# VectorE's stream transpose in place of TensorE's transposes of K and P in a decode block with an 8192-key cache

## The chip, the cores and the metric

One core of one Trainium2 chip runs the whole kernel. The metric is device time in microseconds (us) of one execution. The five engines named below are TensorE (PE in the profile, with PEld for its weight loads), VectorE (DVE), ScalarE (ACT), GpSimd (POOL) and SyncE (SP). Each has its own in-order instruction stream, and they meet through semaphores.

## What is computed

One decode step of a transformer block, for 4 sequences with one new token each. The part that matters here is attention over a cache of 8192 keys for 32 heads of 128 channels:

```python
x: (4, 1, 512); k_cache, v_cache: (4, 32, 8192, 128), all bf16
q = layernorm(x) @ wq                         # per sequence and head: 128 numbers
scores = einsum("bhqd,bhkd->bhqk", q, k_cache) * 128 ** -0.5
p = softmax(scores)
o = einsum("bhqk,bhkd->bhqd", p, v_cache)
h = x + o.reshape(4, 1, 4096) @ wo
out = h + (sigmoid(layernorm(h) @ w_gate) * (layernorm(h) @ w_up)) @ w_down
```

The caches are 128 (sequence, head) pairs of K and V, 2 MB each, 512 MB of K and V in all. Each byte is used once, for one query. "Head" stands for such a pair below, n = 0 to 127.

## The kernel before, in words

**Loads.** SP issues every load (L276 to L304). K or V of one head is one DMA of 2 MB into one of eight slots of the tile `KV` (`NSL`): partition p holds keys 64p to 64p+63, 16 KB in a row. The list `order` (L307 to L314) fixes the sequence: K of head n beside V of head n-9 (`LAGH`), the query weights `wq` behind K 0, four pieces of `wo` behind K 2 to K 5, and the feed-forward weights near and behind the last V. A load into a slot waits until the slot's former holder is used up: a K after its last transpose (`t_tr`), a V after its last product (`t_pv`). `pump` puts loads on SP's queue as soon as that event exists in program order.

**Order of the work.** A loop over u counts quarters of heads (u = 4n + s). In each step it emits the transposes of quarter s of head n, what is due of the softmax chain, the scores of an earlier step, and `pv` of the quarter 36 steps back. Each `emit` appends to one engine's stream with its waits.

**Scores.** The product q.K needs the channels on the partitions, and K arrives with keys there. So `transposes` (L359 to L375) reads K as 32-bit words (two bf16 channels in one word), and TensorE transposes 128x128 words at a time, 32 per head (L364), through four PSUM banks. ScalarE (L373) and VectorE (L375) take turns to copy 128x512 words to the tile `kTc`. `scores` (L377 to L396) then runs, for the even and the odd channel of each word, four products with 32 weight columns each, side by side on the four column strips of the array (L389): 16 for a head. The weights are windows of `Lq`, zero but for q in one column, so that 8 heads (a group, `GH`) collect their scores in different rows of one PSUM bank.

**Softmax.** For each of 16 groups: a copy of the bank to `S_sb` (L403), a maximum over keys (L405, L410 to L425, which go through TensorE for the steps across partitions), the exponential on ScalarE (L427), the sum and the scaling (L433 to L436). Then four TensorE products with the identity transpose P (L443) and VectorE scatters it to `PT` (L451). The chain's steps are emitted 4, 6, 9 and 13 quarter steps behind the group's last scores.

**Output.** `pv` (L458 to L492) multiplies P into V, again on four column strips (L473), for the last group in another form (L485); `finish` and `project` sum the strips (L512, L520) and multiply by `wo` (L502). Behind the loop stand a layer norm and the feed-forward part (L610 to L626) and one small store of the output (L636).

Of the kernel before, what the change touches and what calls it, by code (L numbers as in the profile page):

```python
# [5 lines left out]
BF16 = mybir.dt.bfloat16  # L6
FP32 = mybir.dt.float32
# [5 lines left out]
NTB = 4  # L13
NKT = 8
# [63 lines left out]
def bass_sequential_preLN__mha_block_cached__glu_gated_glu__decode_kernel(  # L78
# [20 lines left out]
    NT = R // 8  # L99
# [4 lines left out]
    W = 64  # L104
# [4 lines left out]
    with ExitStack() as es:  # L109
# [18 lines left out]
        q2 = SB("q2", [128, 2, NH], BF16)  # L128
        Lq = SB("Lq", [128, 2, 2, GH, W], BF16)
        KV = SB("KV", [128, NSL, R * 128], BF16)  # L130
        kTc = SB("kTc", [128, NKT, 512], FP32)
        S_sb = SB("S_sb", [128, 512], FP32)
# [31 lines left out]
        bankT = bank[0:4]  # L164
        SBK, OBK, XS, XO = 4, 5, 6, 7
# [52 lines left out]
        def f_xT(e):  # L218
# [15 lines left out]
            bass.AP(raw(M8), 0, [[GH, 128], [0, 16], [1, GH]])), [t_m8])  # L234

# [110 lines left out]
        t_sev = {}  # L346
# [6 lines left out]
        KVW = KV[:, :, :].bitcast(FP32)  # L353
        kTb = kTc[:, :, :].bitcast(BF16)

        def transposes(n, t):
            g = n * NT + t
            slot = slot_of["k", n]

            def f(e):  # L360
                ins = None
                for i in range(4):
                    c = 128 * (4 * t + i)
                    ins = e.transpose(bankT[g % NTB][:, 128 * i:128 * (i + 1)], KVW[:, slot, c:c + 128], identf[:, :])  # L364
                return ins
            tok = emit("pe", f, [t_k[n][t // 2], t_identf, t_copy.get(g - NTB)])
            if t == NT - 1:
                t_tr[n] = tok

            ks = g % NKT  # L370
            w = [tok, t_score.get(n * 2 + t // 4 - 2)]
            if g % 2 == 0:
                t_copy[g] = emit("act", lambda e: e.copy(kTc[:, ks, :], bankT[g % NTB][:, :]), w)  # L373
            else:
                t_copy[g] = emit("dve", lambda e: e.tensor_copy(kTc[:, ks, :], bankT[g % NTB][:, :]), w)  # L375

        def scores(u):  # L377
            n, m = u // 2, u % 2
            g, i = n // GH, n % GH
            first = i == 0 and m == 0  # L380
            last = i == GH - 1 and m == 1
            off = 31 - (16 * m + i)

            def f(e):
                mms = []
                for par in range(2):
                    for j in range(4):
                        ks = (n * NT + 4 * m + j) % NKT
                        mms.append(e.matmul(PS[32 * j:32 * (j + 1), 512 * SBK:512 * (SBK + 1)],  # L389
                                            Lq[:, g % 2, par, i, off:off + 32], kTb[:, ks, par:par + 1023:2],  # L390
                                            start=first and par == 0, stop=last and par == 1,
                                            tile_position=(0, 32 * j)))
                return mms[4:] if last else mms[-1]
            w = [t_copy[n * NT + 4 * m + j] for j in range(4)] + [t_lq[g]]
            if first and g:
                w.append(t_sev[g - 1])  # L396
            t_score[u] = emit("pe", f, w, incs=4 if last else 1)
# [3 lines left out]
        def softmax(g):  # L401

            t_sev[g] = emit("act", lambda e: e.activation(S_sb[:, :], bank[SBK], ACT.Copy),  # L403
                            [t_score[16 * g + 15], st_.get("exp")])
            t_mx = emit("dve", lambda e: e.tensor_reduce(mpart[:, :], S_sb[:, :], AX.X, ALU.max),  # L405
                        [t_sev[g], st_.get("p1")])
# [14 lines left out]
            def p2():  # L421
                t = emit("pe", lambda e: e.matmul(  # L422
                    bank[XS][:, 128:129], rowpad[:, :], identf[:, 0:1], start=True, stop=True),
                    [box["d2"], t_rp0])
                a1 = emit("dve", lambda e: e.tensor_scalar(  # L425
                    negmb[:, :], bank[XS][:, 128:129], -SCALE, None, op0=ALU.mult), [t, st_.get("exp")])
                box["a2"] = emit("act", lambda e: e.activation(  # L427
                    E_sb[:, :], S_sb[:, :], ACT.Exp, bias=negmb[:, 0:1], scale=SCALE, accum_out=sig[:, 0:1]),
                    [a1, st_.get("ptr")])
                st_["exp"] = box["a2"]  # L430

            def p3():
                t = emit("pe", lambda e: e.matmul(  # L433
                    bank[XS][:, 130:131], Gmat[:, :], sig[:, 0:1], start=True, stop=True), [box["a2"], t_gm])
                d3 = emit("dve", lambda e: e.reciprocal(rsum[:, :], bank[XS][:, 130:131]), [t])
                box["d4"] = emit("dve", lambda e: e.tensor_scalar(  # L436
                    E_sb[:, :], E_sb[:, :], rsum[:, 0:1], None, op0=ALU.mult), [d3, box["a2"]])

            def p4():
                def f(e):  # L440
                    ins = None
                    for q in range(4):
                        ins = e.matmul(bank[XS][:, 128 * q:128 * (q + 1)], E_sb[:, 128 * q:128 * (q + 1)],  # L443
                                       ident[:, :], start=True, stop=True)
                    return ins
                t = emit("pe", f, [box["d4"]])
                st_["ptr"] = t
                pb = g % 2
                dst = bass.AP(raw(PT), pb * NK * GH * 32, [[2 * NK * GH * 32, 128], [GH * 32, NK], [36, GH], [1, 4]])
                src = bass.AP(raw(PS), XS * 512, [[4096, 128], [GH, NK], [1, GH], [128, 4]])  # L450
                st_["xs"] = t_ptc[g] = emit("dve", lambda e: e.tensor_copy(dst, src),  # L451
                                            [t, t_pt0, t_pvg.get(g - 2)])
            return [(4, p1), (6, p2), (9, p3), (13, p4)]

        def pcol(g, i, t, r2):
            kk = 4 * (t % 4) + 2 * (t // 4) + r2
            return g % 2, (kk * GH + i) * 32

        def pv(n, m):
# [5 lines left out]
            if first and g:  # L465
                w.append(t_oev[g - 1])
            if g < NG - 1:
                def f(e):
                    mms = []
                    for j in range(4):  # L470
                        t, r2 = 2 * m + j // 2, j % 2
                        pb, o = pcol(g, i, t, r2)
                        mms.append(e.matmul(PS[32 * j:32 * (j + 1), 512 * OBK:512 * (OBK + 1)], PT[:, pb, o:o + 32],  # L473
                                            in_slot(slot, [[256, 4], [1, 128]], (8 * t + r2) * 128),
# [3 lines left out]
            else:  # L478
                def f(e):
                    ins = None  # L480
                    for r in range(16 * m, 16 * (m + 1)):
                        q = r % 8 // 2
                        pb, o = pcol(g, i, r // 8, r % 2)
                        o += 4 * i + q
                        ins = e.matmul(bank[OBK][:, i:i + 1], KV[:, slot, 128 * r:128 * (r + 1)],  # L485
# [24 lines left out]
        def finish(g):  # L510
            ob = g % 2
            t_oev[g] = emit("act", lambda e: e.activation(O_sb[:, :], bank[OBK], ACT.Copy),  # L512
# [19 lines left out]
        def q_projection():  # L532
# [12 lines left out]
            def f2(e):  # L545
                ins = None
                for par in range(2):
                    for lo in (0, 64):
                        ins = e.matmul(bank[XO][lo:lo + 64, NH * par:NH * (par + 1)], ident[:, par:par + 127:2],
                                       q_all[:, :], start=True, stop=True, tile_position=(0, lo))  # L550
                return ins
            t2 = emit("pe", f2, [tq, t_ident])
            st_["q"] = st_["xo"] = emit("dve", lambda e: e.tensor_copy(
                q2[:, :, :].rearrange("p e n -> p (e n)"), bank[XO][:, 0:2 * NH]), [t2])
# [3 lines left out]
        def q_windows(g):  # L558
            w = [st_["q"], t_lq0, t_score.get(16 * (g - 1) - 1)]
            for r2 in range(2):  # L560
                lo = 64 * r2
                t_lq[g] = emit("dve", lambda e, lo=lo, r2=r2: e.tensor_copy(  # L562
                    Lq[lo:lo + 64, g % 2, :, :, 31 + 8 * r2], q2[lo:lo + 64, :, GH * g:GH * (g + 1)]), w)


        for u in range(4 * (NH + LAGH)):
            n, s = u // 4, u % 4
            for q in range(4):
                if n < NH and q % 2 == 0:
                    transposes(n, 2 * s + q // 2)  # L570
# [6 lines left out]
            if u > 3 and u % 2 == 0 or u == 3:  # L577
                su = u // 2 - 1
                if su < 2 * NH:
                    scores(su)  # L580
                    if su % 16 == 15:
                        if su // 16 + 2 < NG:
                            q_windows(su // 16 + 2)
                        for d, fn in softmax(su // 16):
# [13 lines left out]
        t_ot = emit("dve", lambda e: e.tensor_copy(OT[:, gl % 2, :], bank[OBK][:, 0:GH]),  # L598
# [17 lines left out]
        t_u = emit("pe", glu_mm(t_w["wu"][0], bank[SBK]), [t_hn, t_w["wu"][1], t_sev[gl]])  # L616
        t_hh = emit("dve", lambda e: e.tensor_tensor(hhT[:, :], sg_sb[:, :], bank[SBK][:, 0:NF], ALU.mult), [t_sg, t_u])
# [3 lines left out]
        for i in range(2):  # L621
            def f_down(e, i=i):
                ins = None
                for t in range(half * i, half * (i + 1)):
                    for c in range(NDC):
                        ins = e.matmul(cols(bank[OBK], c), wd_v[:, t, 128 * c:128 * (c + 1)],  # L626
# [5 lines left out]
            h2T[:, :], sth[:, 0:NDC * B], bank[OBK][:, 0:NDC * B], ALU.add), [t_d, st_["h"]])  # L632
# [61 lines left out]
```

## Time and profile before

| | us |
|---|---|
| median of three runs (lowest, highest) | 1312.22 (1311.79, 1312.52) |
| the profiled execution's own time | 1311.99 |
| its span, first to last instruction | 1310.2 |
| TensorE busy | 1029.1, 9293 products and as many weight loads |
| of it, transposes of K (L364) | 664.6, 4096 products |
| VectorE busy | 410.8, 715 instructions |
| ScalarE busy | 335.6, 583 instructions |

Loads move 550.8 MB. The page's rows of engines give the share of the span in which an engine was at work; the row of DMA gives in tenths how busy the 16 DMA engines were in each of 40 slices. "Idle before, releaser" of a group of instructions says how long its engine stood idle ahead of it and what ended that. A granted clock (PEclk) of 1.00 is TensorE's full speed.

### The profile page before, as it was taken

The page shows a single profiled execution, that of the slowest core. Times are in us where ns is not written, and L with a number is a line of the kernel's source. Part 1 is how long each engine was busy: PE and PEld are TensorE (multiplying, and loading weights), DVE is VectorE, ACT ScalarE, POOL GpSimd, SP SyncE. Part 2 cuts the span into 40 slices and gives each one's busy share as a digit, 9 for nine tenths or more (in the row PEclk, how much of TensorE's full clock was granted, in tenths as well). Part 3 has the DMA queues.
Part 4 walks back from the last instruction along what each step waited for, and adds up shares of the span by engine and source line. Part 5 has one row for each costly group of instructions (what it writes and reads, how often), then busy time and mean ns, then how long its engine had stood idle before and what let it go on. Part 6 is the DMA issues. An engine that isn't in the chain of part 4 may idle for free.

```text
span 1310.2 us, 20596 instructions
## 1 busy us (share of the span) xinstructions
PE 1029.1 (79%) x9293; PEld 661.5 (50%) x9293; DVE 410.8 (31%) x715; ACT 335.6 (26%) x583; POOL 9.9 (1%) x11
## 2 busy tenths in 40 slices
PE   5887877887878788878788788787787878878864
PEld 4554544555545455555555455454454555445543
DVE  4442323323233232322323233232232323323310
ACT  1332322222222222222223223222222322222210
POOL 3000000000000000000000000000000000000000
PEclk7998888888888888888888889799798988888865
DMA  9999999999999999999999999999999999999996
GB/s 378 420 426 429 427 428 427 427 428 425 428 427 427 428 427 426 427 429 425 428 427 427 427 427 427 427 429 426 428 426 428 428 427 427 427 428 425 429 421 260
DMA packets 45471, 552.11 MB, mean 421 GB/s; under 512 B 4420, under 2 KB 10312, under 8 KB 12360
## 3 DMA queue, kind: packets, MB, share of 16 engines
q1 hardware_dynamic: 45384, 550.79, 99.3%
q8 instruction: 74, 1.21, 0.4%
q14 instruction: 13, 0.11, 0.0%
HBM read 550.77 MB, written 0.00 MB: 420 GB/s over the span
## 4 chain that ended last, share of the span: by engine, by line
DMA 80%; PE 17%; SPq 2%; ACT 1%; DVE 0%; issue 0%
DMA KV<-in_A_v_cache_dram 75%; PE PS L364 10%; PE PS L473 3%; DMA KV<-in_B_w_down_dram 2%; PE PS L389 2%; DMA KV<-in_A_k_cache_dram 1%; DMA Wreg<-in_A_wq_dram 1%; SPq L279 1%; ACT E_sb L427 0%; DVE kTc L375 0%; SPq L304 0%; PE PS L410 0%; PE PS L433 0%; PE PS L443 0%; PE PS L422 0%
## 5 line engine op out<-in xcount | busy, mean ns | idle before, releaser
L364 PE MATMUL PS<-identf,KV 128*128 128x128 f32 x4096 | 664.6, 311 | 12.8 <-DMA KV<-in_A_k_cache_dram 11.2
L364 PEld LDWEIGHTS PS<-identf,KV 128*128 128x128 f32 x4096 | 518.1, 159 | 192.7 <-issue 152.5
L375 DVE COPY kTc<-PS 128x512 f32<-128x512 f32 x512 | 356.1, 699 | 737.1 <-PE PS L364 736.6
L373 ACT COPY kTc<-PS 128x512 f32<-128x512 f32 x512 | 300.3, 586 | 883.2 <-PE PS L364 883.2
L473 PE MATMUL PS<-KV,PT 128*32 128x512 bf16 x1920 | 215.6, 439 | 223.8 <-DMA KV<-in_A_v_cache_dram 223.8
L473 PEld LDWEIGHTS PS<-KV,PT 128*32 128x32 bf16 x1920 | 51.8, 98 | 346.1 <-DMA KV<-in_A_v_cache_dram 278.8
L389 PE MATMUL PS<-kTc,Lq 128*32 128x512 bf16 x2048 | 177.7, 426 | 1.7 <-DVE Lq L562 1.0
L389 PEld LDWEIGHTS PS<-kTc,Lq 128*32 128x32 bf16 x2048 | 32.2, 97 | 50.4 <-issue 32.0
L485 PE MATMUL PS<-PT,KV 128*128 128x1 bf16 x512 | 15.1, 165 | 17.3 <-DMA KV<-in_A_v_cache_dram 15.1
L485 PEld LDWEIGHTS PS<-PT,KV 128*128 128x128 bf16 x512 | 14.4, 104 | 17.9 <-DMA KV<-in_A_v_cache_dram 15.6
L520 PE MATMUL PS<-selq,O_sb 128*128 128x8 f32 x120 | 16.7, 266 | 3.5 <-ACT O_sb L512 3.5
L520 PEld LDWEIGHTS PS<-selq,O_sb 128*128 128x128 f32 x120 | 15.3, 200 | 7.3 <-ACT O_sb L512 7.3
L451 DVE CAST PT<-PS 128x512 bf16<-128x512 f32 x16 | 11.1, 692 | 23.9 <-PE PS L443 23.9
L427 ACT ACTIVATE E_sb<-S_sb,negmb 128x512 bf16<-128x512 f32 x16 | 11.6, 724 | 22.4 <-DVE negmb L425 22.4
L414 DVE TENSOR_REDUCE mrow<-PS 1x8 f32<-1x128 f32 x16 | 4.5, 278 | 30.9 <-PE PS L410 30.9
L405 DVE TENSOR_REDUCE mpart<-S_sb 128x1 f32<-128x512 f32 x16 | 11.0, 686 | 4.9 <-ACT S_sb L403 4.9
L512 ACT ACTIVATE O_sb<-PS 128x512 f32<-128x512 f32 x15 | 9.0, 598 | 12.0 <-PE PS L473 12.0
L403 ACT ACTIVATE S_sb<-PS 128x512 f32<-128x512 f32 x16 | 9.6, 597 | 9.1 <-PE PS L389 9.1
L598 DVE CAST OT<-PS 128x8 bf16<-128x8 f32 x1 | 0.2, 167 | 32.0 <-PE PS L485 32.0
L207 ACT ACTIVATE lnw<-lnw 128x4 f32<-128x4 f32 x2 | 0.4, 206 | 38.1 <-DVE lnw L204 38.1
L433 PE MATMUL PS<-sig,Gmat 128*128 128x1 f32 x32 | 7.3, 297 | 3.7 <-ACT E_sb L427 3.5
L433 PEld LDWEIGHTS PS<-sig,Gmat 128*128 128x128 f32 x32 | 6.6, 258 | 6.8 <-ACT E_sb L427 6.6
(70 smaller groups left out, 124.8 us busy)
## 6 DMA issues: line engine op xcount, KB each, us to landing
KV<-in_A_k_cache_dram SPq DMA_DIRECT2D x127, 2048.0 KB, 28.3
KV<-in_A_v_cache_dram SPq DMA_DIRECT2D x127, 2048.0 KB, 32.9
Wreg<-in_A_wq_dram SPq DMA_DIRECT2D x4, 1024.0 KB, 11.7
Wreg<-in_A_wo_dram SPq DMA_DIRECT2D x4, 1024.0 KB, 14.6
KV<-in_A_k_cache_dram SPq DMA_DIRECT2D x4, 512.0 KB, 5.7
KV<-in_A_v_cache_dram SPq DMA_DIRECT2D x4, 512.0 KB, 26.1
KV<-in_B_w_gate_dram SPq DMA_DIRECT2D x1, 1792.0 KB, 28.0
KV<-in_B_w_up_dram SPq DMA_DIRECT2D x1, 1792.0 KB, 25.9
```

What stands on the lines that cost most here:

```text
L279: done[n] = [prog.dma("sp", f"sl{slot}", lambda e: e.dma_start(KV[:, slot, :], src), w)] * 4
L364: ins = e.transpose(bankT[g % NTB][:, 128 * i:128 * (i + 1)], KVW[:, slot, c:c + 128], identf[:, :])
L373: t_copy[g] = emit("act", lambda e: e.copy(kTc[:, ks, :], bankT[g % NTB][:, :]), w)
L375: t_copy[g] = emit("dve", lambda e: e.tensor_copy(kTc[:, ks, :], bankT[g % NTB][:, :]), w)
L389: mms.append(e.matmul(PS[32 * j:32 * (j + 1), 512 * SBK:512 * (SBK + 1)], Lq[:, g % 2, par, i, off:off + 32], kTb[:, ks, par:par + 1023:2] ...
L405: t_mx = emit("dve", lambda e: e.tensor_reduce(mpart[:, :], S_sb[:, :], AX.X, ALU.max), [t_sev[g], st_.get("p1")])
L427: box["a2"] = emit("act", lambda e: e.activation(E_sb[:, :], S_sb[:, :], ACT.Exp, bias=negmb[:, 0:1], scale=SCALE, accum_out=sig[:, 0:1]), ...
L433: t = emit("pe", lambda e: e.matmul(bank[XS][:, 130:131], Gmat[:, :], sig[:, 0:1], start=True, stop=True), [box["a2"], t_gm])
L451: st_["xs"] = t_ptc[g] = emit("dve", lambda e: e.tensor_copy(dst, src), [t, t_pt0, t_pvg.get(g - 2)])
L473: mms.append(e.matmul(PS[32 * j:32 * (j + 1), 512 * OBK:512 * (OBK + 1)], PT[:, pb, o:o + 32], in_slot(slot, [[256, 4], [1, 128]], (8 * t ...
L485: ins = e.matmul(bank[OBK][:, i:i + 1], KV[:, slot, 128 * r:128 * (r + 1)], PT[:, pb, o:o + 1], start=(r == 0), stop=(r == R - 1))
L520: ins = e.matmul(bank[XO][:, 0:GH], O_sb[:, 128 * q:128 * (q + 1)], selq[:, q:q + 29:4], start=(q == 0), stop=(q == 3))
```

## The change

K's transposes go to VectorE. Its stream transpose turns blocks of 32x32 words within groups of 32 partitions, from SBUF to SBUF: one instruction takes a quarter of a head, 128x1024 words, straight from the slot to `kTc`, which now has four buffers. PSUM and the two copying engines are no longer on that way. Since the blocks stay in their group of 32 partitions, each group a holds the channels of its own keys: a product needs q repeated in the four groups, each with its own output column. So `Lq` gets windows of 128 columns with four live ones, at 32a + 8s + i for quarter s and head i of the group, and a quarter's scores are four products over the whole array (word half c, channel parity e), 16 for a head as before. `q_windows` now fills two heads at a time with one product by a mask (`amask`); the repeated q comes from a selection matrix (`selrep`). Scores of two groups alternate between two PSUM banks, `S_sb` and its copy go, and the maximum and the exponential read the bank. P's transpose is a stream transpose on VectorE as well, from `E_sb` straight into `PT`. `pv`'s products keep their number and shape; they alternate between two banks and take other rows of V, in the order of the new P. Loads, slots and `order` stay as they are.

```diff
-NTB = 4
-NKT = 8
+NKT = 4
...
+        def transposes(n, s):
+            u = 4 * n + s
+            slot = slot_of["k", n]
+            t_copy[u] = emit("dve", lambda e: e.transpose(
+                kTc[:, u % NKT, :], KVW[:, slot, 64 * RC * s:64 * RC * (s + 1)]), [t_k[n][s], t_score.get(u - NKT)])
+            if s == 3:
+                t_tr[n] = t_copy[u]
...
-                for i in range(4):
-                    c = 128 * (4 * t + i)
-                    ins = e.transpose(bankT[g % NTB][:, 128 * i:128 * (i + 1)], KVW[:, slot, c:c + 128], identf[:, :])
-                return ins
-            tok = emit("pe", f, [t_k[n][t // 2], t_identf, t_copy.get(g - NTB)])
...
-                t_copy[g] = emit("act", lambda e: e.copy(kTc[:, ks, :], bankT[g % NTB][:, :]), w)
-            else:
-                t_copy[g] = emit("dve", lambda e: e.tensor_copy(kTc[:, ks, :], bankT[g % NTB][:, :]), w)
...
+                for ce in range(4):
+                    ins = e.matmul(sbank(g), Lq[:, n // QH % 2, n % QH, ce, off:off + 128],
+                                   k3[:, :, ce // 2, :, ce % 2], start=first and ce == 0, stop=last and ce == 3)
...
-                for par in range(2):
-                    for j in range(4):
-                        ks = (n * NT + 4 * m + j) % NKT
-                        mms.append(e.matmul(PS[32 * j:32 * (j + 1), 512 * SBK:512 * (SBK + 1)],
-                                            Lq[:, g % 2, par, i, off:off + 32], kTb[:, ks, par:par + 1023:2],
...
-            t_sev[g] = emit("act", lambda e: e.activation(S_sb[:, :], bank[SBK], ACT.Copy),
-                            [t_score[16 * g + 15], st_.get("exp")])
-            t_mx = emit("dve", lambda e: e.tensor_reduce(mpart[:, :], S_sb[:, :], AX.X, ALU.max),
-                        [t_sev[g], st_.get("p1")])
+            t_mx = emit("dve", lambda e: e.tensor_reduce(mpart[:, :], sbank(g), AX.X, ALU.max),
+                        [t_score[32 * g + 31], st_.get("p1")])
...
-                    for q in range(4):
-                        ins = e.matmul(bank[XS][:, 128 * q:128 * (q + 1)], E_sb[:, 128 * q:128 * (q + 1)],
-                                       ident[:, :], start=True, stop=True)
...
-                st_["xs"] = t_ptc[g] = emit("dve", lambda e: e.tensor_copy(dst, src),
-                                            [t, t_pt0, t_pvg.get(g - 2)])
+                dst = bass.AP(raw(PT), pb * NK * GH * 32, [[2 * NK * GH * 32, 128], [GH * 32, NK], [1, 4], [36, GH]])
+                t_ptc[g] = emit("dve", lambda e: e.transpose(dst, E_sb[:, :]),
+                                [box["d4"], t_pt0, t_pvg.get(g - 2)])
...
+            t_lq[k] = emit("dve", lambda e: e.tensor_tensor(dst, src, keep, ALU.mult),
+                           [st_["q"], t_lq0, t_am, t_score.get(4 * QH * (k - 1) - 1)])
```

## The prediction, on record before the result was seen

> **What bounds the kernel now.** I read the page's rows of engines and DMA first, since they say whether any engine is full.
>
> ```profile
> PE 1029.1 (79%) x9293; PEld 661.5 (50%) x9293; DVE 410.8 (31%) x715; ACT 335.6 (26%) x583; POOL 9.9 (1%) x11
> ...
> DMA  9999999999999999999999999999999999999996
> ...
> DMA packets 45471, 552.11 MB, mean 421 GB/s; under 512 B 4420, under 2 KB 10312, under 8 KB 12360
> q1 hardware_dynamic: 45384, 550.79, 99.3%
> q8 instruction: 74, 1.21, 0.4%
> ...
> DMA KV<-in_A_v_cache_dram 75%; PE PS L364 10%; PE PS L473 3%; DMA KV<-in_B_w_down_dram 2%; PE PS L389 2%; DMA KV<-in_A_k_cache_dram 1%; DMA Wreg<-in_A_wq_dram 1%; SPq L279 1%; ACT E_sb L427 0%; DVE kTc L375 0%; SPq L304 0%; PE PS L410 0%; PE PS L433 0%; PE PS L443 0%; PE PS L422 0%
> ```
>
> No engine is full; the DMA engines are. The 10% of L364 in the chain is only the way by which a landed slot is handed back to SP. Next, whether a faster hand-back would help: the waits of SP, and the median time from issue to landing.
>
> ```profile
> SPq L279 <- PE PS L473: 1108.4, 120, 14.9
> ...
> SPq L279 <- PE PS L364: 32.8, 12, 9.6
> ...
> KV<-in_A_v_cache_dram SPq DMA_DIRECT2D x127, 2048.0 KB, 32.9
> ```
>
> SP does wait for slots, but what it issues lands 32.9 us later, while the landings of single 2 MB loads follow each other by 4.89 us: some six loads are always queued, so an earlier hand-back only lengthens the queue, and a later one costs nothing until it is some 15 us late (the queue less the lag of the slowest DMA engine, below). One head is a K and a V, so **the period is 9.78 us**.
>
> The same two rows hide what can still move. The table of stages at the end of the span shows a queue that does not drain evenly:
>
> ```profile
> 1280.00:1285.00 5.00, 0.00 (x0) 0.00 (x0) 0.00 (x0) 0.00 (x0) 0.00 (x0) 0.50 1.04 423
> 1285.00:1290.00 5.00, 1.87 (x64) 1.78 (x64) 0.00 (x0) 0.00 (x0) 0.00 (x0) 0.50 0.92 365
> 1290.00:1295.00 5.00, 2.88 (x96) 2.72 (x96) 0.00 (x0) 0.00 (x0) 0.00 (x0) 0.50 0.57 229
> 1295.00:1300.00 5.00, 2.14 (x42) 1.80 (x42) 1.45 (x9) 0.43 (x2) 0.00 (x0) 0.50 0.74 271
> ```
>
> The last two columns are the busy share of the 16 DMA engines and GB/s: in the last 20 us only about half of them work. The trace has 16 landings for each load, one for each DMA engine. Around 20 us they lie within 1.2 us of each other; at 64 us within 2.3 us, at the end within 15 us. By then eight engines lie 12.8 to 15.0 us behind the first, the other eight at most 6.7 us. The packet records say why: queue 8 ("instruction") brings one 16 KB packet about every 18 us, 1.06 us each, where a 16 KB packet of K or V takes 0.613 us. TensorE's stream is 2 x 9293 = 18586 instructions; 1.21 MB is 65 bytes for each, so this is **TensorE's program being fetched**. A single engine's lag jumps by about 1.35 us at such a packet, in turn on eight engines, and never shrinks: the K/V packets take 0.613 us on every engine, and still do when half of the engines have run dry. A load counts as landed with its sixteenth part, so these eight engines set the end: w_down lands at 1306.6 us, and 0.9 us of products, the sum, a small product, a copy and the store follow.
>
> **The change part by part.** TensorE loses 4096 transposes and 64 products for P, each with a weight load: 2 x 4160 = 8320 of 18586 instructions (45%). Scores stay at 2048 and pv at its number. Its program shrinks by 0.542 MB, 33 packets. Price of one: between span times 64 and 1116 us the mean lag of the eight late engines grew from 1.43 to 12.42 us over 57 packets, 0.193 us each, or 6.4 us for 33. By the single jump it is 1.35/8 = 0.169, 5.6 us; by the packet's own 1.06 us alone 0.133, 4.4 us. I take **5.8 us**, near the middle of the upper two, since the jump holds more than the packet. The other engines' lag of 6.7 us caps the gain at 15.0 - 6.7 = 8.3 us. ScalarE's 528 fewer instructions are fetched in 8 KB packets on queue 14, ten in the whole steady part: nothing that ends last.
>
> VectorE drops 512 copies (356.1 us) and gets 512 transposes of 128x1024 words. The trace shows none. The nearest rows:
>
> ```profile
> L375 DVE COPY kTc<-PS 128x512 f32<-128x512 f32 x512 | 356.1, 699 | 737.1 <-PE PS L364 736.6
> L436 DVE TENSOR_SCALAR E_sb<-E_sb,rsum 128x512 bf16<-128x512 bf16 x16 | 5.7, 354 | 0.6
> L228 DVE TENSOR_REDUCE M<-identf 128x8 f32<-128x128 f32 x1 | 0.4, 377 | 0.0
> L543 DVE CAST q_all<-PS 128x128 bf16<-128x128 f32 x1 | 0.3, 291 | 8.2 <-PE PS L537 8.2
> ```
>
> From 128 to 512 words a copy grows by 699 - 291 = 408 ns, 1.06 ns a word, with about 0.155 us fixed: 1.24 us for 1024 words. The quickest row (bf16 from SBUF, 354 ns) gives 0.39 ns an element, so 0.55 us; the slowest per element, the strided reduction, (377 - 155)/128 = 1.73 ns, so 1.93 us. I take 1.24 us, the row of the same words into the same tile, so 5.0 us a head. The rest of VectorE's work: the softmax of a group (0.69 + 0.28 + 0.21 + 0.15 + 0.17 + 0.35 us, some 0.7 for P's scatter, which stays one instruction), 0.33 for the outputs, and four window products of about 0.2 us: 3.7 us for 8 heads. In-order waits within that chain were 1.9 (L414), 1.4 (L435) and 1.5 us (L525) a group. That is 8.5/8 = 1.1 us a head, so VectorE needs 6.1 us of the 9.78 (3.3 to 8.8 by the bounds): hidden by the DMA queue. Its cover is gone where 4T + 1.1 = 9.78, at T = 2.2 us.
>
> The Trainium skill ("VectorE: DVE Perf Modes", The three transpose paths) speaks against the change: it gives 311 ns for a VectorE transpose of 128x128 bf16. Taken eight times for 1024 columns that is an estimate of 2.5 us, 11.1 us a head, and VectorE would bound the kernel. But a 128-column copy already takes 291 ns in this trace, mostly fixed; with 20 ns more for 128 columns the estimate becomes 1.4 us, 6.7 us a head.
>
> TensorE's new scores are 16 whole-array passes of 512 columns a head. A pass over four strips now takes 0.32 us at full clock (eight L389 in 0.64 us) and 0.52 us at half (1.04 us). A whole-array product reads the same columns at the same stride, so I take the same: 5.1 to 8.3 us, with 1.6 to 2.5 us of pv (0.40 or 0.62 us for four L473). Before it was 32 transposes (1.09 or 1.97 us for eight), 4.4 to 7.9 us, with 1.3 to 2.1 of scores and the same pv: 7.3 to 12.5 before, 6.7 to 10.8 after. TensorE gets a little lighter at either clock, and the granted mean is 0.852 now. No gain or loss at the end.
>
> Moved waits: K's slot is now freed by VectorE's fourth transpose. Ahead of it on VectorE stand the maximum (waiting for the group's last scores) and the chain's steps, some 8 us once in eight heads, inside the 15 us that the queue forgives. Behind a transpose that waits for K stand the next softmax steps; all wait for loads in the order of `order`, so none waits for a later one. ScalarE's copy of the scores (0.6 us) leaves the chain, off the path. At the start K 0's transposes end before the last of wq lands (20.3 us), even behind the 5.4 us copy at L232 and the new constants; `wo` waits for the q products as before, with 4 MB of K queued. Sum: 0 at the start, 0 a head, 0 behind the last landing, -5.8 in the lag.
>
> **Rivals.** *The fetch does not decide* (14%): the lag has another source, or the freed time on the eight engines is lost again, since w_down's second half is issued for 16.3 us against a full queue. Then 1311 to 1313 us, that is, unchanged. Against it stands that jumps and packets come one by one. *VectorE becomes the bound* (11%), the other side: a transpose of 32-bit words that needs two passes, 2 x 1.06 x 1024 ns + 0.155 = 2.33 us. Then 10.4 us a head, 0.64 over the period, times some 120 heads behind the first slots: +77 less the 5.8, about 1383 us. It decides from T = 2.2 us on; just above that (2.25 us, 10.1 us a head) it costs 120 x 0.32 = 38 us. For it: no row shows the instruction. Against it: every row of plain 32-bit moves is one pass. A half clock that keeps TensorE at 10.8 us a head is no separate case: before, 12.5 us at half clock did not bind.
>
> **How the numbers follow.** The forecast (75%) is the profiled 1311.99 - 5.8 = 1306.2 us; that execution lies 0.2 us below the median of 1312.22. Its own range is 1303.7 (the cap) to 1308.5 (4.4 us, less a packet's step of about 1 us on the last engine). The range of 8 in 10 adds the no-change case: 1303.5 to 1313. About 0.2%, 2.6 us, is what a measurement of this kernel can tell from no change: faster 0.75, within 0.14, slower 0.11.
>
> **What would show it.** Right: about 41 packets on the instruction queue, the last landings some 8 us apart instead of 15, a DMA share near 1 for longer at the end, VectorE near 680 us (410.8 - 356.1 + 512 x 1.24) and transposes near 1.24 us. Wrong: transposes over 2.2 us, SP waiting for VectorE with a DMA row that shows gaps, or the spread at the end unchanged with fewer packets.

## The result, and the profile after

The changed kernel takes 1307.20 us (median of six, 1306.93 to 1307.51) where the kernel before, on the same chip, takes 1311.82 (1311.58 to 1312.52): a ratio of 0.9964, 95% interval 0.9951 to 0.9977. The profiled execution went from 1311.99 to 1307.25 us, its span from 1310.2 to 1305.1.

The page after: busy time of each engine, DMA packets by queue, and the two new groups of VectorE with the scores of TensorE.

```profile
PE 883.7 (68%) x5133; PEld 283.5 (22%) x5133; DVE 682.3 (52%) x750; ACT 27.4 (2%) x55; POOL 10.3 (1%) x11
...
DMA  9999999999999999999999999999999999999997
...
q1 hardware_dynamic: 45384, 550.79, 99.8%
q8 instruction: 40, 0.66, 0.2%
q14 instruction: 9, 0.07, 0.0%
...
L372 DVE STREAM_TRANSPOSE kTc<-KV 128x1024 f32<-128x1024 f32 x512 | 606.1, 1225 | 446.0 <-DMA KV<-in_A_k_cache_dram 445.1
L391 PE MATMUL PS<-kTc,Lq 128*128 128x512 bf16 x2048 | 650.8, 448 | 14.5 <-DVE kTc L372 12.6
...
L440 DVE STREAM_TRANSPOSE PT<-E_sb 128x512 bf16<-128x512 bf16 x16 | 37.3, 2333 | 0.0
```

The DMA row is as full as before, and SP still waits for slots long before its loads could be late; only the engine that frees a K slot has changed (first lines of SP's waits):

```profile
SPq L293 <- DVE kTc L372: 611.2, 122, 11.9
SPq L293 <- PE PS L461: 494.5, 119, 7.1
```

What has changed is the end. In the table of stages (the last two columns are the busy share of the DMA engines and GB/s) they stay full 5 us longer than before and the uneven rest is short:

```profile
1280.00:1285.00 5.00, 1.87 (x64) 1.78 (x64) 0.00 (x0) 0.00 (x0) 0.00 (x0) 0.50 1.01 416
1285.00:1290.00 5.00, 2.80 (x96) 2.71 (x96) 0.00 (x0) 0.00 (x0) 0.00 (x0) 0.50 1.01 389
1290.00:1295.00 5.00, 2.22 (x45) 1.80 (x42) 1.08 (x7) 0.00 (x0) 0.00 (x0) 0.50 0.83 299
1295.00:1300.00 5.00, 3.79 (x136) 3.71 (x137) 0.77 (x5) 1.71 (x3) 0.00 (x0) 0.50 0.70 235
```

The instruction queue brings 40 packets in place of 74. The sixteen landings of the last quarter of V 127, the last load of the cache, lie 8.6 us apart instead of 14.9. But the first of them comes at 1283.4 us instead of 1281.5: the early engines have become 1.9 us later, and 1.5 us of this is there by 94 us. So w_down lands at 1301.46 instead of 1306.60 us, 5.1 us earlier: 6.3 us won from the lag, 1.9 lost ahead of it, and 0.7 won between this load and w_down. The loss was not in the prediction, so the runs below ask two things: whether the length of TensorE's program is the cause of the gain, and where the loss sits.

### The profile page after: what moved, and what is told of

Read it like the earlier page. It is cut to its first block, busy times and chain, and to the rows that moved or that the text cites. A ratio compares the mean times of both kernels' runs of the same rounds, so it can differ in the third digit from the quotient of the medians.

```text
span 1305.1 us, 11528 instructions
## 1 busy us (share of the span) xinstructions
PE 883.7 (68%) x5133; PEld 283.5 (22%) x5133; DVE 682.3 (52%) x750; ACT 27.4 (2%) x55; POOL 10.3 (1%) x11
## 4 chain that ended last, share of the span: by engine, by line
DMA 84%; PE 13%; SPq 2%; DVE 0%; issue 0%
DMA KV<-in_A_v_cache_dram 80%; PE PS L391 9%; PE PS L461 4%; DMA KV<-in_A_k_cache_dram 1%; DMA KV<-in_B_w_down_dram 1%; SPq L293 1%; DMA Wreg<-in_A_wq_dram 1%; SPq L318 0%; DVE kTc L372 0%; SPq L311 0%; SPq L290 0%; PE PS L473 0%; PE PS L525 0%; PE PS L613 0%; SPq L193 0%
## 5 line engine op out<-in xcount | busy, mean ns | idle before, releaser
L372 DVE STREAM_TRANSPOSE kTc<-KV 128x1024 f32<-128x1024 f32 x512 | 606.1, 1225 | 446.0 <-DMA KV<-in_A_k_cache_dram 445.1
L391 PE MATMUL PS<-kTc,Lq 128*128 128x512 bf16 x2048 | 650.8, 448 | 14.5 <-DVE kTc L372 12.6
L461 PE MATMUL PS<-KV,PT 128*32 128x512 bf16 x1920 | 224.4, 458 | 335.0 <-DMA KV<-in_A_v_cache_dram 335.0
L391 PEld LDWEIGHTS PS<-kTc,Lq 128*128 128x128 bf16 x2048 | 181.4, 109 | 330.1 <-issue 209.1
L549 DVE TENSOR_TENSOR Lq<-q,amask 128x32 bf16<-128x32 bf16 x64 | 18.1, 285 | 41.1 <-PE PS L391 40.8
L440 DVE STREAM_TRANSPOSE PT<-E_sb 128x512 bf16<-128x512 bf16 x16 | 37.3, 2333 | 0.0
L425 ACT ACTIVATE E_sb<-PS,negmb 128x512 bf16<-128x512 f32 x16 | 11.0, 688 | 1153.8 <-DVE negmb L423 1153.8
L508 PE MATMUL PS<-selq,O_sb 128*128 128x8 f32 x120 | 16.7, 266 | 11.7 <-ACT O_sb L500 11.7
L420 PE MATMUL PS<-identf,rowpad 128*128 128x1 f32 x32 | 8.1, 322 | 10.5 <-DVE rowpad L415 10.5
L403 DVE TENSOR_REDUCE mpart<-PS 128x1 f32<-128x512 f32 x16 | 10.9, 683 | 7.2 <-PE PS L391 7.2
L420 PEld LDWEIGHTS PS<-identf,rowpad 128*128 128x128 f32 x32 | 6.7, 261 | 16.6 <-DVE rowpad L415 16.6
```

The lines of the kernel that those rows point to most:

```text
L372: t_copy[u] = emit("dve", lambda e: e.transpose(kTc[:, u % NKT, :], KVW[:, slot, 64 * RC * s:64 * RC * (s + 1)]), [t_k[n][s], t_score.get( ...
L391: ins = e.matmul(sbank(g), Lq[:, n // QH % 2, n % QH, ce, off:off + 128], k3[:, :, ce // 2, :, ce % 2], start=first and ce == 0, stop=last ...
L403: t_mx = emit("dve", lambda e: e.tensor_reduce(mpart[:, :], sbank(g), AX.X, ALU.max), [t_score[32 * g + 31], st_.get("p1")])
L420: t = emit("pe", lambda e: e.matmul(bank[XS][:, 128:129], rowpad[:, :], identf[:, 0:1], start=True, stop=True), [box["d2"], t_rp0])
L425: box["a2"] = emit("act", lambda e: e.activation(E_sb[:, :], sbank(g), ACT.Exp, bias=negmb[:, 0:1], scale=SCALE, accum_out=sig[:, 0:1]), [ ...
L440: t_ptc[g] = emit("dve", lambda e: e.transpose(dst, E_sb[:, :]), [box["d4"], t_pt0, t_pvg.get(g - 2)])
```

## The experiments

Three kernels add instructions of TensorE that nothing needs, one of the kernel before takes some away.

**Eight and sixteen small products.** In each quarter:

```diff
+            if 3 < u < 4 * NH:
+                emit("pe", lambda e: [e.matmul(bank[UBK][:, 0:1], ident[:, :], ident[:, 0:1], start=True, stop=True)
+                                      for _ in range(8)], incs=0)
```

> The changed kernel with eight one-column products of the identity into an unused PSUM bank in each quarter of a head: 4064 products and their weight loads, 8128 instructions, which nothing waits for. Theory (TensorE's program fetch sets the end): the program is again as long as before the change, 32 more 16 KB packets at 0.169 to 0.193 us each, +5.4 to +6.2 us: 1312.6 to 1313.4 us, the last landings about 15 us apart. Rival (the gain came from TensorE's lighter work or from the copies that left ScalarE and VectorE): the products add about 0.1 ms of TensorE time, an eighth of what it has now, to an engine with a third of its time free, so no change, 1307.2 us.

> Sixteen such products in each quarter, 16256 more instructions. Theory: 64 packets, +10.8 to +12.4 us, 1318 to 1319.6 us, on one line with the eight; landings some 20 us apart at the end. Rival: no change as long as TensorE has time left, else a rise that is not in proportion.

Measured: 1313.85 us with eight (ratio to the kernel before 1.0013, 1.0005 to 1.0022) and 1319.80 with sixteen (1.0058, 1.0046 to 1.0071). The packet row of the kernel with eight and of that with sixteen:

```profile
q8 instruction: 71, 1.16, 0.4%
```

```profile
q8 instruction: 103, 1.69, 0.5%
```

Thirty-one packets more cost 6.65 us and 63 cost 12.60, against the changed kernel: 0.21 and 0.20 us each, on one line, and 0.45 and 0.2 us over the ranges expected. The landings of the last quarter of V 127 lie 14.8 us apart with eight, as before the change, and 18.6 with sixteen. The gain is taken back by instructions that do no work.

**One wide product.** Inside `scores`, ahead of the four:

```diff
+                ins = e.matmul(bank[UBK], ident[:, :], k3[:, :, 0, :, 0], start=True, stop=True)
```

> The changed kernel with one whole-array product of 512 columns (the identity on a quarter's kTc) more in each quarter: as much or more TensorE time as the eight small products, about 512 x 0.28 = 143 us, but only 1024 more instructions. Theory: 4 packets, +0.7 to +0.8 us, about 1308. Rival (TensorE's busy time or its reads of SBUF set the pace of the DMA engines): at least as much as eight small products cost.

Measured: 1308.82 us (0.9976, 0.9967 to 0.9986), +1.62. Its rows of engines and of the instruction queue, and then the row of engines with eight small products:

```profile
PE 977.5 (75%) x5645; PEld 333.1 (25%) x5645; DVE 684.3 (52%) x750; ACT 27.4 (2%) x55; POOL 10.3 (1%) x11
...
q8 instruction: 44, 0.72, 0.2%
```

```profile
PE 983.0 (75%) x9197; PEld 392.3 (30%) x9197; DVE 685.8 (52%) x750; ACT 27.4 (2%) x55; POOL 10.3 (1%) x11
```

The same busy time costs a quarter as much when it takes an eighth of the instructions. It is more than the 0.8 expected: the last engine's lag grew by 1.2 us (8.6 to 9.8 at the last quarter of V 127). That is near one jump of 1.35 us, as if one engine had got a whole packet more; this reading was not tested by itself.

**Fewer transposes in the kernel before.**

```diff
-                for i in range(4):
+                for i in range(4 if g < NTB else 1):
```

> The kernel before the change with three of four transposes of K left out (but for the first four tiles); copies, scores and everything else run on what the banks hold, so part of K is not read. 3060 products, 6120 instructions less; VectorE's and ScalarE's work as before. Theory: 24 packets less, -4.1 to -4.6 us against the kernel before, 1307.2 to 1307.7 us, landings about 9 us apart at the end. Rival (the gain of the change came from ScalarE and VectorE, or from the freeing of slots by VectorE): 1311.8 us.

Measured: 1307.34 us (0.9964, 0.9952 to 0.9977), -4.47, inside the expected range, with 24 packets fewer, 0.19 us each; the landings of the last quarter of V 127 lie 10.5 us apart, where about 9 were expected.

```profile
PE 847.0 (65%) x6233; PEld 315.8 (24%) x6233; DVE 408.9 (31%) x715; ACT 334.5 (26%) x583; POOL 9.9 (1%) x11
...
q8 instruction: 50, 0.82, 0.3%
```

VectorE and ScalarE copy as before in it (410.8 and 335.6 us busy in the kernel before), so such a gain does not need what the change took off these two. TensorE is less busy here, as after the change; that this does not matter was shown by the wide product.

**The same on ScalarE.** Eight copies of one column in each quarter, to a tile of their own:

> The changed kernel with eight one-column copies on ScalarE in each quarter, 4064 instructions that nothing waits for, on an engine that is 2% busy: about 0.26 MB of program, 32 packets of 8 KB on queue 14. Theory as far as it goes (any engine's program is fetched by the same DMA engines): if these packets go round eight engines as TensorE's do, 4 more on each, +0.5 us at most; if they fall on one or two, these take 10 to 30 us of lag and end last, 1311 to 1333 us. Rival (only TensorE's stream matters): 1307.2 us.

Measured: 1321.25 us (1.0070, 1.0056 to 1.0084), +14.05, on an engine that is 31% busy:

```profile
q8 instruction: 40, 0.66, 0.2%
q14 instruction: 41, 0.34, 0.1%
```

The landings of V 126 show one DMA engine 22.8 us behind the first and the next at 8.7. So ScalarE's program is fetched by one DMA engine. Its lag grows from 3.45 us at 173 us of the span to 22.8 at 1278, in steps of about 0.7 us, one for each of ScalarE's 8 KB packets; at VectorE's packets on the same queue it has no such step. So 4064 instructions cost twice as much as 8128 of TensorE, whose packets eight engines share.

**VectorE one and a half times, and twice.**

```diff
+            once = emit("dve", lambda e: e.transpose(
+                kTc[:, u % NKT, 0:512], KVW[:, slot, 64 * RC * s:64 * RC * s + 512]), [t_k[n][s], t_score.get(u - NKT)])
...
-                kTc[:, u % NKT, :], KVW[:, slot, 64 * RC * s:64 * RC * (s + 1)]), [t_k[n][s], t_score.get(u - NKT)])
+                kTc[:, u % NKT, :], KVW[:, slot, 64 * RC * s:64 * RC * (s + 1)]), [once])
```

> The changed kernel, in which VectorE transposes half of each quarter of K once more (into the same buffer, ahead of the transpose that counts). Quarters follow each other in 1.16 us on VectorE when nothing holds them, so a head's transposes go from 4.6 to about 7.2 us, and with the 1.2 us of its other work and waits VectorE needs 8.4 of the period of 9.78 us. Theory (VectorE is hidden behind the DMA queue): 1307.2 us, at most 0.8 more where the loads of wo share the time with more transposes. Rival (VectorE's lateness already reaches the slots): about 128 x 2.6 / 2 us or some such large part more, over 1330 us. In the stretch from 20 to 60 us the 1 KB packets of wo, 50 ns each in the changed kernel and 46 before, take over 51 ns if VectorE's transposes slow them.

Measured: 1310.04 us (0.9984, 0.9976 to 0.9993), +2.84, with VectorE 80% busy. Not the large sum of the rival, and more than the 0.8 allowed. The queue still hides the work; the 2.8 us are its program again, 13 packets on queue 14 instead of 9:

```profile
q8 instruction: 40, 0.66, 0.2%
q14 instruction: 13, 0.11, 0.0%
```

One DMA engine falls back by 0.97 us at each of VectorE's packets (2.96 us at 246 us of the span, 11.7 nine packets later). At the last quarter of V 127 it lies at 11.7 us and the next at 9.0, where the last engine of the changed kernel lies at 8.6. The 1 KB packets of wo took 50 ns as in the changed kernel, so more transposes do not slow them.

The second kernel has all 1024 words in place of the 512 above.

> The changed kernel with every quarter of K transposed twice by VectorE: eight transposes of 1.16 us and four waits of about 0.1 us are 9.6 us a head, with its other work 10.8 us, 1.0 over the period. It stands for a transpose of 2.4 us, over the 2.2 us from which the prediction let VectorE bound the kernel. Theory: about 120 heads x 1.0 us more, 1400 to 1450 us, SP waiting for VectorE and gaps in the DMA row. Rival (the queue of eight slots still hides it): under 1320 us.

Measured: 1383.21 us (1.0542, 1.0528 to 1.0557). First the row of engines and the DMA rows of this kernel's page (each digit the busy share, each number GB/s, of a fortieth of the span), then the largest row of SP's waits:

```profile
PE 903.7 (65%) x5133; PEld 285.9 (21%) x5133; DVE 1299.5 (94%) x1262; ACT 27.4 (2%) x55; POOL 10.3 (1%) x11
...
DMA  9997999999999999999999999999999999999996
GB/s 374 408 427 300 426 382 414 419 382 428 381 423 404 398 427 374 425 385 416 415 389 423 377 426 407 390 429 373 425 386 414 417 387 426 378 417 417 385 425 265
```

```profile
SPq L293 <- DVE kTc L374: 1172.0, 125, 11.7
```

Here VectorE bounds the kernel: 10.42 us a head between the landings at 94 and 1345 us (120 heads), 0.64 over the period; expected were 10.8 and over 1400 us. The row of GB/s shows gaps, as the prediction's rival said it would. Nearly all of the lag is gone too (2.4 us at the last quarter of V 127): with a queue that runs empty the early DMA engines have nothing to run ahead with.

**The loss at the start.** Between 20 and 60 us wo's 4096 packets of 1 KB take 46.0 ns each before the change and 50.1 on average after it, and K's 16 KB packets 612 and 622 ns on average: (4096 x 4.1 + 724 x 9.5) ns over 16 engines is 1.5 us. All the kernels above that descend from the changed one have 50, the one with fewer transposes from before has 46. (In the kernel with the copies on ScalarE the new tile puts `Wreg` 96 bytes behind a multiple of 256, with 50.3 ns.) The change moved the tiles in SBUF: `Wreg`, the target of wq and wo, starts at a multiple of 256 bytes in each partition before, and 32 bytes behind one after.

```diff
+        SB("gap", [128, 56], FP32)
         WREG = H * D
```

> The changed kernel with 224 unused bytes ahead of the tile Wreg, so that it starts at a multiple of 256 bytes of SBUF, as it did before the change; in the changed kernel it starts 32 bytes behind one. Theory (the 1 KB packets of wo take 50 instead of 46 ns because their target is not aligned): 46 ns again, the first landings from 90 us on about 1.0 to 1.5 us earlier, 1305.7 to 1306.2 us. Rival (VectorE's transposes or whole-array products slow them): 50 ns and 1307.2 us as before this edit.

> The kernel before the change with 8 unused bytes ahead of Wreg, which moves it 32 bytes off its multiple of 256. Theory (alignment): the 1 KB packets of wo at 50 ns, first landings from 90 us on 1.0 to 1.5 us later, 1312.8 to 1313.3 us. Rival: 46 ns and 1311.8 us.

Measured: 1305.66 us aligned (0.9953, 0.9941 to 0.9966), -1.54, with 46.0 ns; and 1313.44 us for the kernel before with `Wreg` shifted (1.0012, 1.0003 to 1.0021), +1.62, with 50.1 ns. Expected in both directions and measured in both, 0.04 and 0.14 us outside the ranges: 1.5 us of the loss are the place of `Wreg`. With `Wreg` off its boundary in both, the kernel before (74 packets, 1313.44 us) and the changed one with eight small products (71 packets, 1313.85) are 0.4 us apart: the packets and this place explain nearly all of the difference that the change made.

**Both tiles aligned.** `KV` starts 160 bytes behind a multiple of 256 before, and 192 behind one after.

```diff
+        SB("gap0", [128, 16], FP32)
         KV = SB("KV", [128, NSL, R * 128], BF16)
...
+        SB("gap", [128, 40], FP32)
         WREG = H * D
```

> The changed kernel with both Wreg and KV moved to multiples of 256 bytes (KV by 64 bytes, to a multiple of 256; it starts 192 behind one now and started 160 behind one before the change). Theory (a target off its multiple of 256 lengthens each packet by some 4 ns): 4 of 615 ns on the K and V packets, up to 0.6% or 8 us less than 1305.66, and w_down's 1 KB packets at 46 instead of 50 ns; at the least 0.4 us from w_down alone. Rival (K and V packets took 611 ns with an unaligned KV before 76 us in the kernel before, so their later 613 to 620 ns have another cause): 1305.2 to 1305.7 us.

Measured: **1296.38 us** (1296.35 to 1296.54; ratio to the kernel before 0.9881, 0.9864 to 0.9897), 9.3 us less than with `Wreg` alone. The row of GB/s of the kernel with `Wreg` aligned, and of that with both:

```profile
GB/s 380 419 429 427 428 427 429 427 427 429 426 430 426 429 427 428 428 427 427 428 428 428 429 427 429 427 428 427 428 428 427 428 428 427 429 428 425 429 423 303
```

```profile
GB/s 377 420 430 431 431 431 430 431 430 430 431 432 430 430 430 432 431 430 430 430 432 431 430 431 430 431 431 431 429 431 431 431 431 430 429 433 430 430 427 315
```

Of the 40 slices 37 move 1 to 5 GB/s more. Between 300 and 600 us a 16 KB packet takes 611.6 ns on average in place of 615.4 (7861 of 7880 take exactly 611), 0.6% or 7.9 us of the span; TensorE's fetches take 0.94 in place of 1.06 us, and the landings of the last quarter of V 127 lie 7.7 instead of 8.8 us apart. Of w_down's 1792 packets of 1 KB, which go to a slot of `KV`, 1757 take 46 ns in place of 946; their mean stays at 49.9, since 23 of them take over 100 ns at the end. The edit moves the tiles behind `KV` too, `kTc`, `E_sb` and `PT` among them. No load goes to these, and TensorE and VectorE are busy for 888.0 and 683.4 us as against 890.6 and 683.9; but no run moved `KV` alone.

**Eight-partition loads.** Two kernels tried to take bytes from the late engines.

> The changed kernel with the two halves of w_down loaded by 16 DMAs of 8 partitions each instead of one DMA of 128. The Trainium skill (DMA: Bandwidth & Descriptors, Why a DMA increments its semaphore by 16 and not by 1) says that such a DMA uses only eight of the sixteen engines, always the same ones; no run so far shows it. The 1.8 MB are about 5 us of work for eight engines more than their share now. Theory (the lag of the eight engines that fetch TensorE's program decides): if these are the other eight, the late ones have 2.6 us less to move and the end comes 2 to 3 us earlier, 1304 to 1305 us; if they are the late ones, it comes 2.6 to 5 us later, 1310 to 1312 us. Rival (the lag does not decide, or the DMA is spread over all sixteen): 1307 us, plus what the issue of 30 more DMAs costs.

> The changed kernel with Wreg aligned (1305.66 us when run by itself), in which V of head 64 alone is loaded by 16 DMAs of 8 partitions each. If such a DMA uses the same eight of the sixteen engines, these move 128 packets of 16 KB, 16 each, in 9.8 us, and the other eight none of this load in place of 4.9 us. Theory (the lag decides): if the eight are the early ones, the late ones end about 4.9 us earlier and the early ones 4.9 later, all about level, 1301 to 1302 us; if they are the late ones, 4.9 us more, 1310 to 1311 us. Rival (spread over all engines, or the lag does not decide): 1305.7 us.

Measured: 1316.10 us with w_down (1.0034, 1.0022 to 1.0047) and 1323.68 with one V (1.0089, 1.0074 to 1.0104). The second is outside what any theory allowed, the first inside only by the cost of the issue, which had no price. w_down's 32 DMAs took SP 33.8 us to issue, 20.4 for the two in the changed kernel, and the last was issued at 1305 us of the span, when w_down had already landed in the changed kernel (1301.5): the issue set the end. V's sixteen took only 5.4 us to issue, but the core's transfers ran at half rate around their landing:

```profile
690.00:700.00 10.00, 7.02 (x36) 1.92 (x37) 3.19 (x4) 0.00 (x0) 0.00 (x0) 0.83 1.02 431
700.00:720.00 20.00, 8.70 (x54) 3.58 (x49) 10.60 (x14) 1.38 (x3) 0.00 (x0) 0.71 1.02 223
```

From 700 to 720 us a 16 KB packet took 1.19 us on average, where 0.613 is usual; why is open. Of the page's statement (the Trainium skill, DMA: Bandwidth & Descriptors, Why a DMA increments its semaphore by 16 and not by 1) the traces show one half: the sixteen DMAs of V 64 have 128 landings, eight each, where a DMA of 128 partitions has sixteen. Whether these are always the same eight engines, and whether they are the late ones, neither run tells.

## Why the prediction was right, point by point

- **The bound.** The DMA engines stayed full and SP's waits for slots cost nothing, as said. With VectorE one and a half times as long it was still so.
- **The lag.** This step carried the forecast and held. Priced at 5.8 us for 33 packets, it gave 34 fewer packets and 6.3 us at the last quarter of V 127, 0.19 us each. Adding 8128 instructions that do nothing cost 6.65 us; taking away 6120 in the kernel before won 4.47. The rival that the fetch does not decide falls.
- **"At the start 0."** This is the step that failed: it looked at who waits for whom and not at where the tiles lie. A changed list of tiles moved `Wreg` off its boundary, which cost 1.5 us (shown both ways by alignment and shift). The forecast of 1306.2 us for the profiled execution is 1.05 us under the measured 1307.25. At w_down's landing 0.5 us more than forecast came from the lag, 0.7 from w_down itself, and 1.9 were lost by the early engines, of which the place of `Wreg` explains 1.5. The rest of that loss was not traced, nor why w_down lands 5.1 us earlier and the execution ends only 4.7 us earlier. So the total came out closer than its terms, which is luck.
- **VectorE.** The transpose was taken as 1.24 us and has a mean of 1.225 (1.155 when four follow each other, 4.62 us at 38 us of the span). VectorE's busy time was put near 680 us and is 682.3, but this agreement is luck: the terms given for it (410.8 - 356.1 + 512 x 1.24) add up to 690, of which the transposes are 635 and were busy for 606.1, while the rest took 76 in place of 55. The Trainium skill ("VectorE: DVE Perf Modes", The three transpose paths) gives 311 ns for 128x128 bf16. Read as mostly a fixed cost, an estimate of 1.4 us, it comes near the 1.225; the eightfold reading, an estimate of 2.5 us, does not. P's transpose into `PT` was mis-sized, 0.7 against 2.33 us, and the window products, 0.2 against 0.285; both are hidden.
- **TensorE.** A whole-array pass was taken as 0.32 us at full clock. Sixteen take 4.42 us at 39.5 us of the span, but there each four wait for a transpose; between 28.2 and 29.5 us, where none waits, they start 0.22 us apart. So the term was too large by a third, off the path. Its busy time fell from 1029.1 to 883.7 us, which in itself brought nothing, as the wide product shows.
- **The slower rival.** Its condition did not arise, but its price could be measured: with two transposes in each quarter the period became 10.42 us, where 10.4 was worked out for a transpose of 2.33 us, and the time 1383.21 us against 1383. An agreement this close is luck, since that sum keeps the 5.8 us won from a lag that here was nearly gone, and takes P's transpose at 0.7 us. The threshold of 2.2 us was only bracketed, by one and a half transposes and two.

Open is why 16 KB packets already took 611 ns with an unaligned `KV` for the first 76 us of the kernel before, and 613 to 620 ns only later. Alignment removes the later state; what sets it off was not found. The traces narrow it down. Between 20 and 60 us nearly all take 611 ns where `Wreg` is aligned (744 of 764 in the kernel before, 746 of 764 in the changed one with `Wreg` aligned) and nearly none where it is not (10 of 724 in the changed kernel), with an unaligned `KV` in all three. And in the kernel with every quarter transposed twice, whose queue runs empty, 4944 of 7458 take 611 between 300 and 600 us. So an unaligned target alone does not lengthen a 16 KB packet.

## What to carry to other kernels

Where the DMA engines bound a kernel, as here, an engine's instruction count can be a cost even if the engine has time to spare: its program comes through the same DMA engines, and the one that lost most time to it lands last. Read the spread of the sixteen landings of one load, early and late in the span, and the packets of the instruction queues. And after any edit of the list of tiles, look whether the targets of the large loads still start at multiples of 256 bytes: here that was worth 10.8 us, over twice the change itself. Only starts 0, 32, 96, 160 and 192 bytes behind such a multiple were run, so a smaller multiple, 128 bytes, may do.

## What the runs showed of the hardware that was not expected

- TensorE's program is spread over eight DMA engines, 0.19 to 0.21 us of the end for each 16 KB packet; ScalarE's falls on one, about 14 us for 4064 instructions, and VectorE's on one, 2.8 us for 512.
- In a full queue, loads into a tile that starts off a multiple of 256 bytes took longer for each packet: 50.1 against 46.0 ns at 1 KB; 615.4 against 611.6 at 16 KB, with the open point above. With both tiles aligned the kernel takes 1296.38 us, 1.2% less than before the change.
- A stream transpose that scatters single bf16 elements, 72 bytes apart, takes 2.33 us for 512 columns, twice what 1024 dense 32-bit columns take. Whether the element's size or the scatter costs this was not separated.
- Loading one V of 2 MB by sixteen DMAs of 8 partitions cost 18 us (1305.66 to 1323.68).
